# Holding halves of three streamed weight granules in freed PSUM banks, in a recurrent attention kernel

## The chip, the cores and the metric

The kernel runs on 1 core of one Trainium2 chip. The time is device microseconds of one execution on that core; lower is better. A median is over all runs of a kernel in one comparison. A ratio is the mean time of one kernel's fast runs over that of the other's fast runs of the same rounds, so it is not quite the ratio of the medians quoted beside it; the brackets are its 95% interval. Profiles are of single executions. Their spans can lie some way from the median: the profile of before is of a run of 2164.8 us.

## The reference, cut to what matters

```python
def _A_ref(x, mem0, Wq, Wk, Wv, Wo, seg_len):      # x: 1 x 2048 x 1024, 32 heads of 128, bf16
    mem = mem0                                     # 8 rows
    for s in range(n_seg):                         # 64 segments of 32 rows, one after the other
        xs = x[:, s * seg_len:(s + 1) * seg_len, :]
        h = concatenate([mem, xs], axis=1)         # 40 rows
        q, k, v = h @ Wq, h @ Wk, h @ Wv           # 1024 -> 32 x 128
        p = softmax(where(mask, q @ k.T * scale, -1e9))
        o = (p @ v) @ Wo                           # 4096 -> 1024
        mem = o[:, :M, :]                          # the next segment needs these rows
        outs.append(o[:, M:, :])
    return concatenate(outs, axis=1)
# result = x + _A_ref(layernorm(x), ...) + _B_ref(layernorm(x), ...)
# _B_ref: two rows picked by a router go through a gated MLP; it makes up the tail
```

The recurrence sets the form of the kernel: every segment needs the eight memory rows of the one before, so all four weight matrices are gone through 64 times.

## The kernel before

The weights are 64 granules of 128 x 2048 bf16 (512 KB): six phases of eight for Q, K and V (each matrix in two halves of heads), then sixteen for Wo. 42 granules stay resident in SBUF. The other 22 are streamed anew in each segment through six slots. The transfer that refills a slot is issued when TensorE has used the slot's granule.

```python
PHASES = [(0, 0), (1, 0), (0, 1), (1, 1), (2, 0), (2, 1)]       # (Q, K or V; half of the heads)
streamed = set(((2 * i + 1) * NG) // (2 * n_str) for i in range(n_str))
psA = ...bufs=2 ("acc");  psL = ...bufs=2 ("accl");  psT, psS one bank each;  psO = two banks ("otp")

def fetch():                                                    # called when a granule is used up
    t = wstream.tile([P, 2048], BF16, tag="g", name="g")        # one of six slots
    nc.sync.dma_start(out=granule_out(t, what[1]), in_=granule_dram(what[1]))
...
for p, (mat, half) in enumerate(PHASES):
    PSm = psA.tile(...)                                         # accumulator of the 24 new rows + 8 memory rows
    PSl = psL.tile(...) if mat in left else None                # accumulator of left rows
    for kc in range(KC):
        Gv = granule(8 * p + kc)
        # 4 matmuls of 512 columns into PSm; 4 more into PSl where there are left rows
        used(8 * p + kc)
        for fn in hooks.pop((p, kc), []): fn()                  # smaller work hung in after a granule
```

The last eight rows of each segment ("left rows") are gathered over four segments, so that one pass serves 32 of them. By j, the number of a segment modulo 4: segments with j = 0 have the V matmuls of left rows and seven deferred granules of their output projection (WL), j = 2 and 3 have their Q and K, j = 3 begins WL, and j = 1 has none of this but the preparation of the next group's input rows. The output of a group of left rows is finished in the next j = 0 segment by three hooks. Their input rows XL use the one buffer with the tag "vm", which also holds OB, the output of the segment before, until its stores have landed.

```python
def load_left(G, queue=nc.gpsimd):
    X = one.tile([P, 512], BF16, tag="vm", name="XL")           # waits until the stores of OB have landed
    ...four transfers from x...
OB = one.tile([P, 512], BF16, tag="vm", name="OB")
...
todo += [((1, 3), left_load), ((3, 6), left_norm), ((4, 3), left_store)]   # (phase, granule of the phase)
```

`left_norm` normalises XL on VectorE. `left_store` adds it to WL on TensorE (the "residual"), copies WL out and stores it. Attention of a half of the heads (`scores`, softmax, `attend`) is hung in after granules (2,5), (4,5), (5,3), (5,6) and inside the output projection.

## Time and profile before

The median was 2148.7 us at first, and 2149.8 us (2137.5 to 2168.0) over four runs, the first three and one more. The lines of the page, of TensorE's waits and of the windows are in the prediction. Cutting the trace where ScalarE has copied OB out gives this table by kind of segment (means of 15 or 16 segments; "granules" is TensorE's idle time ended by a streamed granule, "other" all its other idle time of that sort; sums of the trace):

| j | us a segment | TensorE busy | waits: granules | waits: other | MB moved |
|---|---|---|---|---|---|
| 0 | 32.35 | 27.46 | 1.25 | 3.19 | 11.7 |
| 1 | 30.50 | 23.86 | 4.15 | 2.21 | 12.0 |
| 2 | 31.69 | 26.10 | 2.49 | 2.84 | 12.0 |
| 3 | 31.71 | 27.57 | 0.47 | 3.77 | 12.4 |

One more line of before is from the waits of VectorE (who waited for whom: us in total, times, longest), at the normalisation of XL:

```profile
DVE XL L254 <- DMA QKL<-qkl_d: 20.8, 16, 3.2
```

(As the prediction says, the name in this line is a wrong guess: what lands is XL.) So left rows came a little late, 1.3 us on average in 16 waits.

### The profile page before, as it was taken

The page shows a single profiled execution, that of the slowest core. Times are in us where ns is not written, and L with a number is a line of the kernel's source. Part 1 is how long each engine was busy: PE and PEld are TensorE (multiplying, and loading weights), DVE is VectorE, ACT ScalarE, POOL GpSimd, SP SyncE. Part 2 cuts the span into 40 slices and gives each one's busy share as a digit, 9 for nine tenths or more (in the row PEclk, how much of TensorE's full clock was granted, in tenths as well). Part 3 has the DMA queues.
Part 4 walks back from the last instruction along what each step waited for, and adds up shares of the span by engine and source line. Part 5 has one row for each costly group of instructions (what it writes and reads, how often), then busy time and mean ns, then how long its engine had stood idle before and what let it go on. Part 6 is the DMA issues. An engine that isn't in the chain of part 4 may idle for free.

```text
span 2163.1 us, 81861 instructions
## 1 busy us (share of the span) xinstructions
PE 1741.4 (81%) x36202; PEld 897.5 (41%) x36202; DVE 730.2 (34%) x2196; ACT 503.6 (23%) x1165; POOL 544.5 (25%) x1030
## 2 busy tenths in 40 slices
PE   3588888887888888788888888888888888878775
PEld 1234444444444444444444444444444444444341
DVE  5533332333333333333333333333333333233330
ACT  4512222212222222221222122222222222222220
POOL 4422212222132222223122221323222222322211
PEclk8689998999999999999999989999999999999996
DMA  9899999999999999999999999999999999999998
GB/s 359 331 387 382 384 363 352 369 364 383 369 369 393 358 379 399 386 394 386 393 380 392 375 382 386 381 398 373 389 396 389 401 372 400 369 392 350 380 381 345
DMA packets 294344, 818.22 MB, mean 378 GB/s; under 512 B 37458, under 2 KB 42770, under 8 KB 293988
## 3 DMA queue, kind: packets, MB, share of 16 engines
q1 hardware_dynamic: 267652, 782.34, 95.1%
q0 software_dynamic: 23520, 26.06, 3.6%
q8 instruction: 283, 4.64, 0.8%
q10 hardware_dynamic: 2816, 4.59, 0.6%
q14 instruction: 73, 0.60, 0.1%
HBM read 800.22 MB, written 12.59 MB: 376 GB/s over the span
## 4 chain that ended last, share of the span: by engine, by line
DMA 42%; PE 42%; DVE 6%; issue 5%; ACT 3%; POOL 2%; ACTq 0%; POOLq 0%; DVEq 0%; SPq 0%
PE PSm L563 19%; DMA g<-in_A_Wo_dram 14%; DMA g<-in_A_Wv_dram 10%; PE PSl L567 6%; DMA g<-in_A_Wq_dram 6%; PE WO L603 5%; DMA qkl_d<-QS 3%; PE WL L603 3%; PE PTq L422 2%; DMA g<-in_A_Wk_dram 1%; PE OP L512 1%; DVE SPS L472 1%; DMA XP<-in_A_x_dram 1%; DVE NM L471 1%; DMA wres<-in_A_Wo_dram 1%
## 5 line engine op out<-in xcount | busy, mean ns | idle before, releaser
L563 PE MATMUL PSm<-wres,ST 128*32 128x512 bf16 x8192 | 756.7, 399 | 22.3 <-DVE ST L302 17.9
L563 PE MATMUL PSm<-g,ST 128*32 128x512 bf16 x4096 | 422.3, 399 | 69.2 <-DMA g<-in_A_Wk_dram 25.6
L563 PEld LDWEIGHTS <-ST 128*32 128x32 bf16 x12288 | 301.0, 98 | 411.3 <-issue 170.7
L603 PEld LDWEIGHTS <-OT 128*32 128x32 bf16 x8192 | 214.8, 97 | 157.0 <-issue 139.0
L575 ACT CAST XB<-PSm 128x512 bf16<-128x512 f32 x256 | 150.4, 588 | 542.3 <-PE PSm L563 542.3
L603 PE MATMUL WO<-wres,OT 128*32 128x256 bf16 x5120 | 231.9, 278 | 15.0 <-issue 9.1
L603 PE MATMUL WO<-g,OT 128*32 128x256 bf16 x3072 | 160.3, 278 | 92.2 <-DMA g<-in_A_Wo_dram 70.0
L567 PE MATMUL PSl<-wres,STL 128*32 128x512 bf16 x2048 | 208.7, 397 | 0.0
L333 POOL DMA_DIRECT2D QKL<-qkl_d x126 | 91.9, 730 | 329.8 <-PE SPS L466 131.5
L517 ACT CAST OT<-OP 128x256 bf16<-128x256 f32 x256 | 95.4, 373 | 247.8 <-PE OP L514 247.8
L473 ACT ACTIVATE SPS<-SPS 128x320 f32<-128x320 f32 x128 | 54.0, 422 | 397.4 <-DVE SPS L472 386.5
L636 POOL DMA_DIRECT2D out_dram<-OB x256 | 129.6, 513 | 66.0 <-DVE OB L632 37.1
L422 PE MATMUL PTq<-IDENT,XB 128*128 128x128 bf16 x1024 | 103.1, 224 | 48.4 <-ACT XB L575 37.2
L454 POOL COPY KT<-QKL 128x128 bf16<-128x128 bf16 x128 | 38.3, 299 | 383.1 <-PE WO L603 301.5
L471 DVE TENSOR_REDUCE NM<-SPS 128x8 f32<-128x320 f32 x128 | 62.9, 491 | 205.6 <-PE SPS L466 205.6
L519 DVE CAST OTL<-OP 128x64 bf16<-128x64 f32 x128 | 28.7, 224 | 296.9 <-ACT OT L517 296.9
L422 PEld LDWEIGHTS <-XB 128*128 128x128 bf16 x1024 | 60.0, 98 | 152.9 <-ACT XB L575 126.6
L567 PEld LDWEIGHTS <-STL 128*32 128x32 bf16 x3072 | 84.7, 100 | 67.7 <-issue 12.7
L512 PE MATMUL OP<-PT,VM 32*128 32x40 bf16 x2048 | 92.4, 178 | 24.7 <-ACT VM L585 23.0
L512 PEld LDWEIGHTS <-VM 32*128 32x128 bf16 x2048 | 64.8, 91 | 112.0 <-ACT VM L585 49.3
L429 DVE COPY KT<-PTq 128x512 bf16<-128x512 bf16 x128 | 54.2, 424 | 164.3 <-PE PTq L422 162.7
L567 PE MATMUL PSl<-g,STL 128*32 128x512 bf16 x1024 | 104.2, 396 | 0.0
(133 smaller groups left out, 1951.3 us busy)
## 6 DMA issues: line engine op xcount, KB each, us to landing
g<-in_A_Wq_dram SPq DMA_DIRECT2D x384, 512.0 KB, 7.2
g<-in_A_Wo_dram SPq DMA_DIRECT2D x384, 512.0 KB, 7.2
g<-in_A_Wk_dram SPq DMA_DIRECT2D x320, 512.0 KB, 6.5
g<-in_A_Wv_dram SPq DMA_DIRECT2D x320, 512.0 KB, 8.0
qkl_d<-QS POOLq DMA_DIRECT2D x64, 128.0 KB, 5.9
QKL<-qkl_d POOLq DMA_DIRECT2D x126, 64.0 KB, 5.8
g<-in_B_w_gate_dram SPq DMA_DIRECT2D x16, 448.0 KB, 6.9
g<-in_B_w_up_dram SPq DMA_DIRECT2D x16, 448.0 KB, 5.8
```

Of the source, the lines that this page charges most:

```text
L333: nc.gpsimd.dma_start(out=t[:, :, :], in_=qkl_d[s // 4][:, half, :, s % 4, :].rearrange("m p c -> p m c"))
L422: nc.tensor.transpose(out=PTq[:, il, :, :].rearrange("p j r -> p (j r)"), in_=XB[:, il * P:(il + 1) * P], identity=IDENT[:, :])
L429: nc.vector.tensor_copy(out=keys(half)[:, :, 0:32], in_=pv)
L471: nc.vector.tensor_reduce(out=NM[:, :], in_=S8, axis=AX.X, op=ALU.max, negate=True)
L473: nc.scalar.activation(out=S8, in_=S8, func=ACTF.Exp, scale=SCALE)
L512: nc.tensor.matmul(o, lhsT=VM[half][q0:q0 + 32, il * P:(il + 1) * P], rhs=PTm[q0:q0 + 32, il, 0:NK], start=True, stop=False, tile_position ...
L517: nc.scalar.copy(out=OT[half][:, 2 * ph:2 * ph + 2, :, :], in_=ov[:, :, :, 0:SEG])
L563: nc.tensor.matmul(PSm[32 * jq:32 * jq + 32, :], lhsT=ST[:, kc, :], rhs=Gv[:, 512 * jq:512 * (jq + 1)], start=(kc == 0), stop=(kc == KC - ...
L567: nc.tensor.matmul(PSl[32 * jq:32 * jq + 32, :], lhsT=cur["stl"][:, kc, :], rhs=Gv[:, 512 * jq:512 * (jq + 1)], start=(kc == 0), stop=(kc ...
L575: nc.scalar.copy(out=XB[:, :], in_=PSm[:, :])
L603: nc.tensor.matmul(PS[32 * g:32 * g + 32, 0:256], lhsT=lhs(h), rhs=Gv[:, D * hs + 256 * g:D * hs + 256 * (g + 1)], start=(first and hs == ...
L636: nc.gpsimd.dma_start(out=out2[s * SEG:s * SEG + XM, 256 * g:256 * (g + 1)], in_=OB[32 * g:32 * g + XM, 0:256])
```

## The change

Its intent: save transfers. Three of the four PSUM banks that attention sums and left rows had used separately are freed, each keeps half a granule (256 KB) for the whole run, and ScalarE copies it into the slot while only the other half is transferred. To free the banks, the attention sums go into the accumulator's bank and the transposes' bank, and left rows get one bank where they had two. With one bank, WL must be out before phase 4 begins, so its normalisation and store come earlier. The diff, cut to its core (the prologue's and tail's renaming of banks is left out):

```diff
+HELD = (18, 27, 36)
...
-    psL = ...bufs=2;  psO = ...bufs=1 (two banks)
+    psL = ...bufs=1;  psC = ...bufs=1 (three banks, c0 to c2)
...
-            if what[0] == "w":
+            if what[0] == "w" and what[1] in held:
+                nc.sync.dma_start(out=t[:, 0:1024], in_=granule_dram(what[1])[:, 0:1024])
+                nc.scalar.copy(out=t[:, 1024:2048], in_=held[what[1]][:, :].bitcast(BF16))
+            elif what[0] == "w":
                 nc.sync.dma_start(out=granule_out(t, what[1]), in_=granule_dram(what[1]))
...
+            ends.append(lambda: softmax(half, S8, NM))      # exponent behind the phase's accumulator copy
+
+        def softmax(half, S8, DN):
             nc.scalar.activation(out=S8, in_=S8, func=ACTF.Exp, scale=SCALE)
...
-            OP = psO.tile([P, 2, 512], F32, tag="otp", name="OP")
+            if ph == 0:
+                OA[half] = psA.tile([P, 512], F32, tag="acc", name="OA")
+            OB1 = psT.tile([P, 4 * NK], F32, tag="t", name="OP")
+            c1 = 256 if half == 0 else 256 * ph
+            OP = (OA[half][:, c1:c1 + 4 * NK], OB1[:, :])
...
+            lag, behind = 2 if j == 0 else 0, []            # left matmuls two granules behind
...
+                if s == 0 and g in HELD:
+                    held[g] = psC.tile([P, 512], U32, tag=f"c{HELD.index(g)}", name="HELD")
+                    nc.vector.tensor_scalar(out=held[g][:, :], in0=Gv[:, 1024:2048].bitcast(U32), ...)
...
-        WO = psA.tile([P, 512], F32, tag="acc", name="WO")
+        WO = OA[0]
...
-            todo += [((1, 3), left_load), ((3, 6), left_norm), ((4, 3), left_store)]
+            todo += [((1, 3), left_load), ((2, 4), left_norm), ((3, 4), left_store)]
```

More of the change, by code (lines that the diff above doesn't have):

```diff
@@ L71 @@
     streamed = set(((2 * i + 1) * NG) // (2 * n_str) for i in range(n_str))
+    assert all(g in streamed and g < 48 for g in HELD)
     def granule_dram(g):
@@ L90 @@
     psA = ctx.enter_context(tc.tile_pool(name="psA", bufs=2, space=PSUM))
-    psL = ctx.enter_context(tc.tile_pool(name="psL", bufs=2, space=PSUM))
+    psL = ctx.enter_context(tc.tile_pool(name="psL", bufs=1, space=PSUM))
     psT = ctx.enter_context(tc.tile_pool(name="psT", bufs=1, space=PSUM))
     psS = ctx.enter_context(tc.tile_pool(name="psS", bufs=1, space=PSUM))
-    psO = ctx.enter_context(tc.tile_pool(name="psO", bufs=1, space=PSUM))
+    psC = ctx.enter_context(tc.tile_pool(name="psC", bufs=1, space=PSUM))
     qkl_d = [dram.tile([2, 2, P, 4, P], BF16, name=f"qkl_d{t}") for t in range(NT)]
@@ L196 @@
     res_tiles = {}
+    held = {}
     def fetch():
@@ L397 @@
             VL = one.tile([P, 1024], BF16, tag="vl", name="VL")
-        QT, KT, QKL, PTs, OT, nxt = {}, {}, {}, {}, {}, {}
+        QT, KT, QKL, PTs, OT, OA, nxt = {}, {}, {}, {}, {}, {}, {}
         hooks = {}
+        ends = []
         def hook(p, kc, fn):
@@ L472, in scores @@
             nc.vector.tensor_tensor(out=S8, in0=S8, in1=NM[:, :].unsqueeze(2).to_broadcast([P, 8, NK]), op=ALU.add)
+            ends.append(lambda: softmax(half, S8, NM))
+        def softmax(half, S8, DN):
             nc.scalar.activation(out=S8, in_=S8, func=ACTF.Exp, scale=SCALE)
-            DN = NM
             nc.vector.tensor_reduce(out=DN[:, :], in_=S8, axis=AX.X, op=ALU.add)
@@ L510, in attend @@
                     c0 = half * 512 + il * P
-                    o = OP[:, jl, il * NK:(il + 1) * NK]
+                    o = OP[jl][:, il * NK:(il + 1) * NK]
                     nc.tensor.matmul(o, lhsT=VM[half][q0:q0 + 32, il * P:(il + 1) * P], rhs=PTm[q0:q0 + 32, il, 0:NK],
@@ L515, in attend @@
                                      start=False, stop=True, tile_position=(q0, 0), skip_group_check=True)
-            ov = OP[:, :, 0:4 * NK].rearrange("p a (i q) -> p a i q", i=4)
-            nc.scalar.copy(out=OT[half][:, 2 * ph:2 * ph + 2, :, :], in_=ov[:, :, :, 0:SEG])
             h0 = 16 * half + 8 * ph
-            (nc.scalar.copy if half == 0 else nc.vector.tensor_copy)(
-                out=OTL[:, h0:h0 + 8, j, :].rearrange("p (a i) r -> p a i r", a=2), in_=ov[:, :, :, SEG:NK])
+            for jl in range(2):
+                ov = OP[jl].rearrange("p (i q) -> p i q", i=4)
+                copy = nc.vector.tensor_copy if half == 1 and jl == 1 else nc.scalar.copy
+                copy(out=OT[half][:, 2 * ph + jl, :, :], in_=ov[:, :, 0:SEG])
+                copy(out=OTL[:, h0 + 4 * jl:h0 + 4 * jl + 4, j, :], in_=ov[:, :, SEG:NK])
         for pk, fn in todo:
@@ L564 @@
                                      start=(kc == 0), stop=(kc == KC - 1), tile_position=(0, 32 * jq))
-                if PSl is not None:
+                if s == 0 and g in HELD:
+                    held[g] = psC.tile([P, 512], U32, tag=f"c{HELD.index(g)}", name="HELD")
+                    nc.vector.tensor_scalar(out=held[g][:, :], in0=Gv[:, 1024:2048].bitcast(U32), scalar1=0, scalar2=None,
+                                            op0=ALU.bitwise_or)
+                if PSl is None:
+                    used(g)
+                else:
+                    behind.append((kc, Gv))
+                while behind and (len(behind) > lag or kc == KC - 1):
+                    kl, Gl = behind.pop(0)
                     for jq in range(4):
-                        nc.tensor.matmul(PSl[32 * jq:32 * jq + 32, :], lhsT=cur["stl"][:, kc, :],
-                                         rhs=Gv[:, 512 * jq:512 * (jq + 1)], start=(kc == 0), stop=(kc == KC - 1),
+                        nc.tensor.matmul(PSl[32 * jq:32 * jq + 32, :], lhsT=cur["stl"][:, kl, :],
+                                         rhs=Gl[:, 512 * jq:512 * (jq + 1)], start=(kl == 0), stop=(kl == KC - 1),
                                          tile_position=(0, 32 * jq))
-                used(g)
+                    used(8 * p + kl)
                 for fn in hooks.pop((p, kc), []):
@@ L583 @@
                 c0 = half * 512
+                if PSl is not None:
+                    nc.scalar.copy(out=VL[:, c0:c0 + 512], in_=PSl[:, :])
                 VM[half] = one.tile([P, 512], BF16, tag="vm", name="VM")
                 nc.scalar.copy(out=VM[half][:, :], in_=PSm[:, :])
-                if PSl is not None:
-                    nc.scalar.copy(out=VL[:, c0:c0 + 512], in_=PSl[:, :])
+            while ends:
+                ends.pop(0)()
         assert not hooks
@@ L679 @@
         for fh in range(2):
-            GU[w, fh] = (psA, psL)[w].tile([P, 512], F32, tag=("acc", "accl")[w], name="GU")
+            GU[w, fh] = psA.tile([P, 512], F32, tag="acc", name="GU") if w == 0 else \
+                psC.tile([P, 512], F32, tag=f"c{fh}", name="GU")
         for kc in range(KC):
@@ L710 @@
     nc.vector.tensor_copy(out=HT[:, :, :, :], in_=PTh.rearrange("p i (q r) -> p i q r", q=4)[:, :, :, 0:2])
-    YP = psO.tile([P, 2, 512], F32, tag="otp", name="YP")
+    YP = [psC.tile([P, 512], F32, tag="c2", name="YP"), psL.tile([P, 512], F32, tag="accl", name="YP")]
     for i in range(FC // 2):
@@ L717 @@
             for dh in range(2):
-                nc.tensor.matmul(YP[0:2, dh, :], lhsT=HT[:, 4 * fh + b, q, :],
+                nc.tensor.matmul(YP[dh][0:2, :], lhsT=HT[:, 4 * fh + b, q, :],
                                  rhs=Gt[:, a * D + dh * 512:a * D + (dh + 1) * 512],
@@ L722 @@
     NEW = fin.tile([2, D], BF16, name="NEW")
-    nc.vector.scalar_tensor_tensor(out=NEW.rearrange("p (a d) -> p a d", a=2), in0=YP[0:2, :, :], scalar=SIG[:, 0:1],
-                                   in1=OUTR.rearrange("p (a d) -> p a d", a=2), op0=ALU.mult, op1=ALU.add)
+    for dh in range(2):
+        c = slice(512 * dh, 512 * (dh + 1))
+        nc.vector.scalar_tensor_tensor(out=NEW[:, c], in0=YP[dh][0:2, :], scalar=SIG[:, 0:1], in1=OUTR[:, c],
+                                       op0=ALU.mult, op1=ALU.add)
     for c in range(2):
```

## The prediction

> **What bounds the kernel now.** I read the page from the top, then the chain of waits, the waits of TensorE, and windows cut where one segment's output is copied out. The page first:
>
> ```profile
> span 2163.1 us, 81861 instructions
> PE 1741.4 (81%) x36202; PEld 897.5 (41%) x36202; DVE 730.2 (34%) x2196; ACT 503.6 (23%) x1165; POOL 544.5 (25%) x1030
> ...
> DMA  9899999999999999999999999999999999999998
> ...
> q1 hardware_dynamic: 267652, 782.34, 95.1%
> ...
> DMA 42%; PE 42%; DVE 6%; issue 5%; ACT 3%; POOL 2%; ACTq 0%; POOLq 0%; DVEq 0%; SPq 0%
> ```
>
> The transfer engines are nearly always busy, 95.1% of them with the weight queue. Yet the chain that ended last is split evenly between transfers and TensorE, so both limits are close. How often TensorE itself waits for a streamed granule is in its waits (who waited for whom: us, times, longest):
>
> ```profile
> PE WO L603 <- DMA g<-in_A_Wo_dram: 70.0, 124, 1.8
> ...
> PE PSm L563 <- DMA g<-in_A_Wk_dram: 25.6, 52, 1.8
> ...
> PE PSm L563 <- DMA g<-in_A_Wv_dram: 21.2, 47, 1.2
> ...
> PE PSm L563 <- DMA g<-in_A_Wq_dram: 18.1, 40, 1.4
> ```
>
> These sum to 134.9 us in 263 waits: direct waiting is only 6% of the span. The windows give 115.6 us up to the end of segment 0, 1987.6 us for the other 63 segments (381 GB/s) and 59.9 us for the tail: 31.55 us a segment. Four segments in a row, j = 0, 1, 2, 3 (columns: stretch, us, busy and count of PE, PEld, DVE, ACT, POOL, clock, DMA share, GB/s):
>
> ```profile
> 1477.60:1508.70 31.10, 26.77 (x612) 14.73 (x603) 10.30 (x33) 7.49 (x18) 10.50 (x21) 1.00 1.00 356
> 1508.70:1539.90 31.20, 23.51 (x481) 11.47 (x481) 10.90 (x34) 6.16 (x16) 8.15 (x17) 1.00 1.03 401
> 1539.90:1570.40 30.50, 25.41 (x547) 13.16 (x547) 10.10 (x31) 7.65 (x18) 6.58 (x14) 1.00 1.01 378
> 1570.40:1599.50 29.10, 26.59 (x597) 14.32 (x598) 10.86 (x31) 7.24 (x17) 6.48 (x14) 1.00 1.03 412
> ```
>
> The j = 1 segment moves 401 GB/s: transfers set its pace. The j = 0 segment, which has left rows and deferred projections, moves only 356: there TensorE sets it. Averaged over all segments of a kind the windows give 32.4, 30.5, 31.7 and 31.7 us.
>
> [...] VectorE's half of OB waits for ScalarE's half of the same bank 32 times, 124.5 us. [...]
>
> **The change, part by part.**
>
> Held halves. Of 22 granules of 512 KB a segment streams, three come as 256 KB. 3 x 0.262 = 0.786 MB less a segment; a segment now moves 1987.6 x 381 / 63 = 12.02 MB, so 6.5% less. Rows become 2 KB rather than 4 KB; Wo already has 2 KB rows, and its granules land in 7.2 us, as those of Wq do, so I charge nothing. At today's 381 GB/s 11.23 MB take 29.5 us, at 400 they take 28.1. If transfers alone mattered: 2.07 x 63 = 130 us saved.
>
> Copies. From 266 ns for 128 columns (OB) and 588 for 512 (XB) a column costs 0.84 ns: 588 + 512 x 0.84 = 1.02 us each, 3.1 us a segment, about 195 us more on ScalarE, which is busy 23%: 32% after it. They are issued after granules 1, 10 and 18, that is at kc 1, 2 and 2 of phases 0, 1 and 2, five or more granules ahead of the next accumulator copy. A granule takes TensorE 0.22 us when fed (starts of successive groups in the timeline), so 1.1 us are there: these copies should hardly delay anything.
>
> Attention sums. Each attend had two evacuations (373 and 218-224 ns) and gets four of some 266 and 191 ns (my estimate for 32 columns from the same slope). For half 0 all four are on ScalarE: 0.91 us in place of 0.59; the second attend, three granules later, may wait some 0.3 us. WO now lies in the bank that ScalarE is still reading for half 0, so its residual waits for the first two of these copies, some 0.4 us. Half 1 gets shorter, as both engines copy. Together 0 to 0.7 us a segment on TensorE, 0.2 where it sets the pace on average; nothing where transfers do.
>
> Exponent behind the accumulator copy. It frees XB by up to 0.4 us in phases 2 and 4; the wait of the transposes for XB is 37.2 us in all. I take 15 us back, 0.2 us a segment, which cancels the line above.
>
> Left rows with one bank. This is the part I fear. WL must be out before phase 4, so the normalisation moves from granule (3,6) to (2,4) and the store from (4,3) to (3,4), but the load stays at (1,3). Its transfers cannot start until the four OB stores have landed, since both use one buffer. POOL and VectorE in that j = 0 segment, and when TensorE begins scores of half 0, the hook after (2,4) (start, us, engine, line):
>
> ```profile
> 1478.19 2.03 POOL L636 DMA_DIRECT2D out_dram<-OB  x4 [0.55 <-DVE OB L632]
> ...
> 1485.23 2.00 POOL L245 DMA_DIRECT2D XL<-in_A_x_dram  x4 [3.30 <-PE PSm L563]
> ```
>
> ```profile
> 1493.70 0.28 DVE L254 TENSOR_SCALAR XL<-XL,SC 128x256 bf16<-128x256 bf16 x1 [1.89 <-DMA QKL<-qkl_d]
> ```
>
> ```profile
> 1486.52 0.19 PE L461 MATMUL SPS<-KT,QT 128*32 128x40 bf16 x4
> ```
>
> The XL rows land about 15.6 us into the segment (loads at 1485.2 to 1486.7, up to 6.7 us to landing), and VectorE already waits 1.9 us for them (the name QKL in the bracket is a wrong guess; the load of XL is what lands then). After the change it waits from about 1486.3, some 7 us, with the maxima of half 0 and the copies of Q and K queued behind. TensorE reaches (3,4) at about 1489.9 and needs the normalised rows: it stops until some 1494.9, 5 us. Then VectorE works off the softmax of half 0 (3.7 us: 0.49, 0.50, the exponent 0.55, 0.49, 0.20, 0.42, 0.21, 0.43, 0.40) before Q of half 1, so the transposes at (4,1) stop for another 2 us. From (4,1) to the end took 15 us with 1.7 us of waits. So j = 0 costs about 34.5 us, 2 to 3 more than now, in 15 segments. j = 1 has such a load too, but its normalisation stays at (3,6); it can't fall much below 27 us.
>
> **The sum.** TensorE's side: 31.55 less the 134.9 / 63 = 2.1 us of waits for granules gives 29.4 us; a wait also adds the tail of an isolated group to busy time (0.40 us alone, 0.22 in a row): 263 x 0.18 / 63 = 0.7 us, so 28.7. XL adds 6 us of stop in one of four segments: +1.4, of which slower-paced phases hide a little: about 29.9. The transfers' side: 28.1 to 29.5. Six slots, some 8 us of lead, let transfers run on while TensorE stands, so the two add up only partly; two limits so close never reach either, and I take 30.3 us. Saved: 1.25 x 63 = 79 us. Prologue (three VectorE copies, one left bank) and tail: unchanged within 3 us. 2148.7 - 79 = 2070 us.
>
> **Rivals.** (a) Transfers alone bound it and the stops hide in the slots' lead: 130 us saved, 2019 us. For it: DMA share 1.00 and more in most segments, and a stop of 7 us is shorter than the lead. Against it: 361 GB/s on average in j = 0 segments. (b) TensorE and its feeders bound it: the three copies, the XL stop and shared banks eat the gain, and TensorE's waits for granules turn into waits for XL and Q: 10 to 40 us saved, 2110 to 2140. For it: direct waits are only 135 us, and j = 3 segments have hardly any (0.5 us). (c) The in-order ScalarE becomes the feeder that is late: a held copy waits for its slot, and XB behind it. Against it: the copy follows the very granule that frees the slot, and ScalarE has three quarters of its time free; I give it little.
>
> **Range and chances.** Between (a) near-complete and the mild end of (b): 2030 to 2110. The 2% line is at 2105.7. Faster 0.86, same 0.13, slower 0.01.
>
> **What would show it.** Weight queue 782 to about 733 MB (3 x 63 x 0.262 = 49.5). A row of 189 ScalarE copies of about 1.02 us. VectorE's waits ahead of XL in j = 0 growing to some 6 us each, about 90 us in all, and TensorE waiting on POOL's XL at the residual of WL, 3 to 5 us each, where it is 5.4 us in all now. j = 0 segments near 34.5 us, j = 1 near 27.5, the others near 29 to 30. TensorE's direct waits for granules falling from 135 to 50 us or less. The prediction is wrong if 2 KB rows lower the rate, if XL lands much earlier than 15 us into the segment, if the slots' lead swallows the stops (a), or if held copies delay XB.

## The result, and the profile after

The changed kernel took 2217.1 us (2210.0 to 2227.9, four runs) beside 2149.8 us for the kernel before: ratio 1.031 [1.022, 1.040], **slower by 3.1%**. Executions over 1.5% slower than the fastest of the same kernel are left out of the means. The prediction was 2070, with 2030 to 2110. Its outputs passed the comparison.

The page of after, the lines that answer to those of before (span; engines; DMA share in forty slices; weight queue with packets, MB and share; the chain that ended last):

```profile
span 2208.3 us, 82817 instructions
...
PE 1764.8 (80%) x36202; PEld 900.5 (41%) x36202; DVE 752.3 (34%) x2328; ACT 705.9 (32%) x1738; POOL 543.0 (25%) x1030
...
DMA  9899999989999999999999999999999999899989
...
q1 hardware_dynamic: 267652, 732.79, 90.8%
...
PE 42%; DMA 38%; DVE 7%; issue 6%; ACT 4%; POOL 3%; ACTq 0%; DVEq 0%; POOLq 0%; SPq 0%
```

The bytes fell by 49.5 MB as planned, ScalarE rose to 32% as planned, and the span still grew. In the chain POOL went from 2 to 3%, VectorE from 6 to 7%. The waits of TensorE name what is new (us in total, times, longest):

```profile
PE OA L632 <- DMA g<-in_A_Wo_dram: 70.1, 127, 1.8
PE WL L302 <- POOL XL L263: 47.4, 14, 7.6
...
PE PSm L581 <- DMA g<-in_A_Wq_dram: 26.9, 39, 2.0
...
PE PSm L581 <- DMA g<-in_A_Wk_dram: 8.8, 22, 1.2
...
PE PSm L581 <- DMA g<-in_A_Wv_dram: 5.5, 14, 0.9
```

The residual of WL waits 47.4 us for normalised left rows, where it was 5.4. The waits for granules sum to 111.3 us, where they were 134.9; those in the output projection did not move (70.0 and 70.1). VectorE waits for the same rows ahead of that:

```profile
DVE XL L261 <- DMA XL<-in_A_x_dram: 67.5, 19, 8.7
```

The four segments that the prediction showed, after the change (stretch, us, busy and count of PE, PEld, DVE, ACT, POOL, granted clock, DMA share, GB/s):

```profile
1501.90:1536.30 34.40, 28.98 (x620) 15.27 (x608) 10.60 (x35) 10.72 (x27) 10.34 (x21) 0.88 0.86 285
1536.30:1567.70 31.40, 24.58 (x481) 11.55 (x481) 11.22 (x36) 9.32 (x25) 8.13 (x17) 0.95 1.02 378
1567.70:1600.00 32.30, 26.96 (x548) 13.64 (x548) 10.70 (x33) 10.92 (x28) 6.68 (x14) 0.95 0.96 351
1600.00:1631.30 31.30, 26.98 (x606) 15.06 (x610) 10.91 (x32) 10.35 (x26) 6.37 (x13) 0.97 1.01 383
```

Two things are to be seen. The j = 0 segment (first line) has become the longest, its clock fell to 0.88 and its transfers to 285 GB/s. And the other three did not get clearly shorter, though each moves fewer bytes: the rate fell with the bytes. Averaged over all segments:

| j | before, us | after, us | predicted, us | clock before, after | waits for granules before, after |
|---|---|---|---|---|---|
| 0 | 32.35 | 35.10 | 34.5 | 0.98, 0.91 | 1.25, 0.58 |
| 1 | 30.50 | 30.69 | 27.5 | 0.95, 0.95 | 4.15, 4.01 |
| 2 | 31.69 | 31.51 | 29 to 30 | 0.98, 0.97 | 2.49, 1.89 |
| 3 | 31.71 | 31.96 | 29 to 30 | 0.96, 0.95 | 0.47, 0.37 |

The difference of the spans is 2208.3 - 2163.1 = 45.2 us. The segments account for it: 15 x 2.75 = 41.3 from j = 0, and 16 x (0.19 - 0.18 + 0.25) = 4.2 from the rest. The medians are 67 us apart, so this pair of profiles shows two thirds of the measured loss; the other 22 us, 0.35 us a segment, are not in the table.

Now the stop itself, in the first of those four segments. First POOL's issues of the XL load, then VectorE at the normalisation, then TensorE (start, us, engine, line, operation, and in brackets the idle time before it and what ended it):

```profile
1509.67 0.98 POOL L252 DMA_DIRECT2D XL<-in_A_x_dram  x2
```

```profile
1511.76 0.16 DVE L260 RECIPROCAL SC<-SC 128x1 f32<-128x1 f32 x1
1516.80 0.29 DVE L261 TENSOR_SCALAR XL<-XL,SC 128x256 bf16<-128x256 bf16 x1 [4.88 <-DMA XL<-in_A_x_dram]
```

```profile
1518.21 0.41 PE L302 MATMUL WL<-XL,IDENT 128*32 128x256 bf16 x4 [3.81 <-POOL XL L263]
1518.38 0.66 PE L581 MATMUL PSm<-wres,ST 128*32 128x512 bf16 x4
```

The last two XL transfers are issued at 1509.67, VectorE waits 4.88 us for them, normalises, POOL adds, and TensorE has stood for 3.81 us. VectorE's maxima of half 0 stand behind that wait: their scores were done at 1512.3, and they ran at 1517.33. The second TensorE line has something that I had not expected: a group of four matmuls takes 0.66 us, where isolated groups took 0.40. Windows of 2 us across the stop show why (columns as above; the last three are the granted clock, DMA share and GB/s):

```profile
1513.90:1515.90 2.00, 0.51 (x8) 0.10 (x5) 0.00 (x0) 0.00 (x0) 0.00 (x0) 1.00 0.96 323
1515.90:1517.90 2.00, 0.00 (x0) 0.11 (x1) 1.03 (x4) 0.00 (x0) 0.40 (x1) 0.78 1.02 398
1517.90:1519.90 2.00, 1.69 (x20) 0.86 (x23) 1.37 (x4) 0.71 (x2) 1.85 (x5) 0.50 0.93 371
1519.90:1521.90 2.00, 1.49 (x16) 0.55 (x12) 1.32 (x6) 0.58 (x1) 1.88 (x4) 0.50 0.61 127
1521.90:1523.90 2.00, 2.00 (x24) 0.66 (x22) 0.41 (x1) 0.00 (x0) 0.00 (x0) 0.51 0.59 206
1523.90:1525.90 2.00, 2.00 (x65) 1.11 (x61) 0.65 (x2) 0.00 (x0) 0.35 (x1) 1.00 0.48 109
```

The clock granted to TensorE falls to half during the stop and stays there until about 1523.9. In both traces it is either 1.00 or 0.50 and changes only on a grid of 3.41 us (they list 74 stretches of it for before, 122 for after). So a mean of 0.78 in the second window means that 44% of its 2 us were at half: the half clock began near 1517.0 and lasted some 6.8 us, two steps of the grid. TensorE did not have to stand for a whole step to lose its clock: the half clock began 2.6 us into the stop, after a step in which TensorE was still busy for 0.80 of 3.41 us. Two steps of after, then two of before, at a place where no stop of TensorE is longer than 1.35 us (columns as above):

```profile
1513.61:1517.02 3.41, 0.80 (x12) 0.44 (x9) 0.22 (x1) 0.00 (x0) 0.00 (x0) 1.00 0.99 348
1517.02:1520.43 3.41, 2.22 (x24) 0.86 (x23) 2.71 (x9) 1.15 (x3) 2.78 (x6) 0.50 0.83 330
```

```profile
1883.68:1887.09 3.41, 1.99 (x26) 0.77 (x23) 0.85 (x3) 0.58 (x1) 0.66 (x1) 1.00 1.01 338
1887.09:1890.51 3.42, 3.42 (x32) 1.23 (x35) 0.42 (x1) 0.59 (x1) 1.69 (x4) 0.50 1.02 417
```

With the 63 segments of both traces cut into such steps, full clock went over to half 86 times, and each time TensorE had been busy for 1 to 59% of the step before; no step at full clock with more was followed by half, while some with as little as 46% were not either. So a stop of some 1.5 us, or a few short ones, can cost the clock here (an estimate from these shares: 41% of a step is 1.4 us). In all, these segments had 130 us at half clock before and 239 after, of which 24 and 92 in j = 0.

The DMA share shows the other half of the damage: while TensorE stands and crawls, no slot comes free, and the transfers fall to 0.61, 0.59 and 0.48 of their share. The six slots did not carry them over the stop.

And the row of held copies, as predicted (busy, mean ns of one; idle before them):

```profile
L220 ACT COPY g<-HELD 128x1024 bf16<-128x1024 bf16 x189 | 191.2, 1012 | 259.4 <-PE PSm L581 169.8
```

### The profile page after: what moved, and what is told of

Read it like the earlier page. It is cut to its first block, busy times and chain, and to the rows that moved or that the text cites.

```text
span 2208.3 us, 82817 instructions
## 1 busy us (share of the span) xinstructions
PE 1764.8 (80%) x36202; PEld 900.5 (41%) x36202; DVE 752.3 (34%) x2328; ACT 705.9 (32%) x1738; POOL 543.0 (25%) x1030
## 3 DMA queue, kind: packets, MB, share of 16 engines
q1 hardware_dynamic: 267652, 732.79, 90.8%
## 4 chain that ended last, share of the span: by engine, by line
PE 42%; DMA 38%; DVE 7%; issue 6%; ACT 4%; POOL 3%; ACTq 0%; DVEq 0%; POOLq 0%; SPq 0%
PE PSm L581 21%; DMA g<-in_A_Wo_dram 13%; DMA g<-in_A_Wq_dram 9%; PE PSl L594 7%; PE OA L632 4%; DMA XL<-in_A_x_dram 4%; DMA qkl_d<-QS 3%; DMA g<-in_A_Wv_dram 2%; PE PTq L430 2%; PE WL L632 2%; DMA XP<-in_A_x_dram 1%; ACT XB L602 1%; POOL XL L252 1%; PE SPS L474 1%; DMA out_dram<-OB 1%
## 5 line engine op out<-in xcount | busy, mean ns | idle before, releaser
L581 PE MATMUL PSm<-wres,ST 128*32 128x512 bf16 x8192 | 774.6, 409 | 20.4 <-DVE ST L309 17.9
L581 PE MATMUL PSm<-g,ST 128*32 128x512 bf16 x4096 | 428.8, 407 | 44.2 <-DMA g<-in_A_Wq_dram 26.9
L220 ACT COPY g<-HELD 128x1024 bf16<-128x1024 bf16 x189 | 191.2, 1012 | 259.4 <-PE PSm L581 169.8
L632 PE MATMUL OA<-wres,OT 128*32 128x256 bf16 x5120 | 235.2, 277 | 26.2 <-issue 20.9
L632 PE MATMUL OA<-g,OT 128*32 128x256 bf16 x3072 | 159.0, 278 | 74.0 <-DMA g<-in_A_Wo_dram 70.1
L535 ACT CAST OT<-OA 128x128 bf16<-128x128 f32 x256 | 67.9, 265 | 227.7 <-PE OP L529 226.3
L430 PE MATMUL PTq<-IDENT,XB 128*128 128x128 bf16 x1024 | 106.3, 229 | 43.0 <-ACT XB L602 28.1
L594 PEld LDWEIGHTS <-STL 128*32 128x32 bf16 x3072 | 87.3, 101 | 91.8 <-issue 35.1
L614 ACT CAST VM<-PSm 128x512 bf16<-128x512 f32 x128 | 77.4, 604 | 140.6 <-PE PSm L581 140.6
L535 DVE CAST OT<-OP 128x128 bf16<-128x128 f32 x128 | 37.3, 291 | 224.4 <-PE OP L529 224.4
```

The costliest lines, as they stand in the source:

```text
L220: nc.scalar.copy(out=t[:, 1024:2048], in_=held[what[1]][:, :].bitcast(BF16))
L430: nc.tensor.transpose(out=PTq[:, il, :, :].rearrange("p j r -> p (j r)"), in_=XB[:, il * P:(il + 1) * P], identity=IDENT[:, :])
L535: copy(out=OT[half][:, 2 * ph + jl, :, :], in_=ov[:, :, 0:SEG])
L581: nc.tensor.matmul(PSm[32 * jq:32 * jq + 32, :], lhsT=ST[:, kc, :], rhs=Gv[:, 512 * jq:512 * (jq + 1)], start=(kc == 0), stop=(kc == KC - ...
L594: nc.tensor.matmul(PSl[32 * jq:32 * jq + 32, :], lhsT=cur["stl"][:, kl, :], rhs=Gl[:, 512 * jq:512 * (jq + 1)], start=(kl == 0), stop=(kl ...
L614: nc.scalar.copy(out=VM[half][:, :], in_=PSm[:, :])
```

## The experiments

Two questions: is the stop the whole loss, and where did the saved transfers go? Fifteen kernels ran; each was compared with the kernel before on its own chip (medians of before: 2146.6, 2149.4, 2150.0 and 2157.2 us, in the order of the four groups below). All but e4, e10, e11, e13, e14 and e15 compute the reference. Those six are wrong; the comparison of outputs passed them as well, so its tolerance does not see such edits.

### First group: the stop and the halves apart

**e1** keeps the whole change, but gives OB another buffer, so that XL can be loaded at once at the start of the j = 0 segment.

```diff
-        OB = one.tile([P, 512], BF16, tag="vm", name="OB")
+        OB = one.tile([P, 512], BF16, tag="pt", name="OB")
-            todo += [((1, 3), left_load), ((2, 4), left_norm), ((3, 4), left_store)]
+            todo += [((0, 1), left_load), ((2, 4), left_norm), ((3, 4), left_store)]
```

> The change whole, but the output rows OB sit in another buffer, so that the left rows of the j = 0 segments are loaded at granule (0,1) rather than after the stores have landed; the stop at the residual of WL should go. Theory A (the stop, and the halved TensorE clock after it, are the whole loss, and the held halves gain next to nothing): 2110 to 2155 us, j = 0 segments from 35.1 to 31.5 us or so. Theory B (the halves are worth the forecast 80 us, and the stop ate them): 2060 to 2100. Theory C (copies or 2 KB rows cost time of their own): 2165 to 2200, j = 1 to 3 unchanged.

Measured: 2129.8 us, 0.991 [0.988, 0.994] of before. The residual's wait for XL is gone from TensorE's waits, VectorE has no wait for XL at all, and j = 0 takes 31.27 us at a clock of 0.97, down from 35.10 at 0.91. Against the changed kernel that is 0.991 / 1.031, or 3.9% less. The late left rows are the loss (e6 below shows that a small part of this gain was to be had before the change too).

**e2** holds nothing and keeps the stop; **e3** is e1 and holds nothing.

```diff
-HELD = (18, 27, 36)
+HELD = ()
```

> The change with no granule held: full transfers, no ScalarE copies, the stop still there. A: within 1% of the changed kernel, 2200 to 2235, as the halves neither gain nor cost. B: slower than the changed kernel by 30 us or more. C: faster than it by 25 us or more.

> Both edits: no stop and nothing held. A: within 1% of the early-load run, 2110 to 2160. B: slower than the early-load run by 40 us or more. C: faster than it by 25 us or more.

Measured: e2 2239.5 us, 1.040 [1.033, 1.047]; e3 2146.7 us, 1.001 [0.998, 1.003]. So the halves gain 2239.5 - 2217.1 = 22 us beside the stop and 2146.7 - 2129.8 = 17 us without it. They do gain, but a sixth to an eighth of the 130 us that the saved transfer time would have been.

**e6** is the kernel before with the early load of e1 alone (its normalisation stays where it was).

> The kernel before with the same early load of left rows in j = 0. VectorE waited there 1.3 us a segment for these rows, 20.8 us in all; TensorE waited 5.4 us. A, B, C alike: 0 to 15 us faster than before. If it is faster by over 30 us, left rows were already a bound before and part of the early-load run's gain is not the undoing of the change.

Measured: 2129.1 us, 0.993 [0.989, 0.997]. The 20.8 us of waits shown above were worth most of their size to the kernel before.

With these four the loss can be followed step by step, in ratios to before: loading XL early in the kernel before -0.7% (e6); the rest of the change without held halves, early load, +0.8% (e3 over e6); the held halves -1.0% (e1 over e3); the load put back to its late place +4.0% (after over e1). Together they make +3.1% by construction, since each step starts where the last one ends; what the runs tell is the size of each.

### Second group: what swallowed the halves' gain

**e4** tests whether the copies eat the gain. It is e1 with the half transfers and without ScalarE's copies; TensorE reads the transferred half twice instead (wrong).

```diff
-                nc.scalar.copy(out=t[:, 1024:2048], in_=held[what[1]][:, :].bitcast(BF16))
+                    cq = jq % 2 if s > 0 and g in HELD else jq      # first half read twice
```

> Wrong result on purpose. The early-load run with three granules of 256 KB, without the ScalarE copies: TensorE reads the loaded half twice. A: the copies hide; within 0.7% of the early-load run (2115 to 2145). C (copies cost time of their own): 2085 to 2110.

Measured: 2141.2 us, 0.998 [0.995, 1.000]. Without the copies it is not faster than e1 (0.991). The copies cost nothing that can be seen. But e4 lies only 0.3% under e3 (1.001), where e1 lies 1.0% under it: the 17 us of gain are uncertain by a good part of themselves.

**e7** is e1 and also loads the left rows of the j = 1 segment early, at (0,1) in place of (1,3).

> The early-load run with the j = 1 load of left rows early too, at granule (0,1). VectorE waits there for these rows at (3,6). A: 0 to 20 us faster than the early-load run, as the transfers set j = 1. If left rows hold up j = 1 as they did j = 0 after the change: 30 us or more faster.

Measured: median 2146.2 us, ratio 0.994 [0.991, 0.998]. One run of 2114.0 us lies far below the others, which makes ten of the twenty count as slow by the 1.5% rule; by the medians of all runs it is 2146.2 to 2149.4. There is no further gain: in j = 1 the left rows were not late.

**e10** asks what the transfers are worth at all. It is e3, but all 22 streamed granules are transferred by half after their first time, and the half is read twice (wrong).

```diff
+            elif what[0] == "w" and what[1] in seen:
+                nc.sync.dma_start(out=t[:, 0:1024], in_=...first half...)
```

> Wrong result on purpose. The early-load run with nothing held, but from segment 1 on all 22 streamed granules come as 256 KB and TensorE reads their first half twice: the same instructions, half the streamed bytes (5.8 MB less a segment), no copies. Theory A (TensorE and what feeds it set the pace almost as tightly as transfers): 2030 to 2100 us, that is 45 to 115 below its base of 2147. Theory B (transfers are the bound, the halves' gain was lost elsewhere): under 1900. If A, the waits for granules are gone and others stay: issue, Q and K copies, the turn of a segment.

Measured: 1871.2 us, 0.872 [0.867, 0.877], with 419 MB in place of 782 on the weight queue and its share at 68%. TensorE's waits for streamed granules of the four attention matrices fall from 161.3 us in e3 to 3.4. Its segments take 27.78, 24.26, 28.76 and 26.96 us for j = 0 to 3, 2.9 to 6.2 us less than in the kernel before: TensorE with its other feeders can go that much faster in every kind. What matters more is which other waits went as well. These are TensorE's waits called "issue" (time in which it waited for nothing that the profile shows) in e3 and in e10, one fence each:

```profile
PE OA L632 <- issue: 19.6, 19, 2.4
...
PE WL L632 <- issue: 14.8, 12, 2.9
```

```profile
PE OA L641 <- issue: 4.9, 11, 0.8
...
PE WL L641 <- issue: 3.6, 6, 0.8
```

Nothing but bytes was taken away, and issue waits fell from 39.9 to 9.8 us in all. They depend on transfers, then. The page of before has a queue for instructions (packets, MB, share of the 16 engines):

```profile
q8 instruction: 283, 4.64, 0.8%
```

TensorE ran 72,404 matmuls and weight loads, which is 256 to each of these 283 packets of 16 KB, and all 52 of its issue waits in that trace end 1.2 to 1.6 us after such a packet has landed (median 1.35). The reading: TensorE's instructions come in these packets, through the same busy engines, and where it runs through them fastest, in the output projection with eight matmuls and eight weight loads a granule, it runs out of them. In the trace of before sixteen matmuls of 256 columns took 0.61 us there, as eight of 512 columns did elsewhere, and 44.9 of TensorE's 55.8 us of issue waits are in the projection.

**e11** tests that. It is e6 with the projection written as four matmuls of 512 columns in place of eight of 256: the same columns and bytes, half the instructions (wrong).

```diff
-            for hs in range(2):
-                for g in range(4):
-                    nc.tensor.matmul(PS[..., 0:256], lhsT=lhs(2 * w + hs), rhs=Gv[:, D * hs + 256 * g:...])
+            for g in range(4):
+                nc.tensor.matmul(PS[..., 0:512], lhsT=lhs(2 * w), rhs=Gv[:, 512 * g:512 * (g + 1)])
```

> Wrong result on purpose. The kernel before with the early load, and the output projection issued as four matmuls of 512 columns a granule in place of eight of 256: the same columns streamed through TensorE, 64 matmuls and 64 weight loads fewer a segment and as many fewer for left rows. Each wait of TensorE named issue in the trace ends some 1.3 us after the landing of a 16 KB instruction fetch. If these fetches pace the dense stretches: waits named issue fall from 50 us to 15 or less and the run is 40 us or more faster than its base of 2129. If they only fill slack: under 15 us faster.

Measured: 2098.3 us, 0.976 [0.971, 0.982], which is 31 us under e6 by the medians, or 36 by the ratios (0.9930 - 0.9764 of 2149.4). Every issue wait has gone from TensorE's waits (54.0 us in e6), while TensorE's busy time fell by 7.0 us only (1727.5 to 1720.5; its weight loads, which overlap, by 138.5). On this reading the fetch of instructions costs some 30 us in this kernel; the run also takes away half of the projection's weight loads and can't tell the two apart by time alone. Of the 54.0 us, 31 came back as waits for granules (131.5 us in e6, 162.5 in e11).

### Third group: place, softmax, row length, and the early normalisation alone

**e9** is the kernel before with two hooks moved and nothing else.

```diff
-            todo += [((1, 3), left_load), ((3, 6), left_norm), ((4, 3), left_store)]
+            todo += [((1, 3), left_load), ((2, 4), left_norm), ((3, 4), left_store)]
```

> The kernel before, with one part of the change alone: the normalisation of left rows moved from (3,6) to (2,4) and their store from (4,3) to (3,4). If the stop on the left rows is the cause of the loss by itself, the kernel before slows by 40 to 100 us (2190 to 2250), j = 0 segments go from 32.4 to 35 us or more, and TensorE waits for POOL's XL some 4 us in each. If the loss needs the other parts too (shared banks, copies), it stays under 2175.

Measured: 2227.5 us in the median of four runs, 1.036 [1.031, 1.041] by the three fast ones. One line of the old kernel costs as much as the whole change did (1.031 [1.022, 1.040]). Its profiled run fell in the slow state, so only its names are read, not its times: VectorE waits for XL as in the changed kernel, and TensorE stands at the next transposes, behind VectorE's softmax.

```profile
DVE XL L254 <- DMA XL<-in_A_x_dram: 88.4, 19, 9.2
```

```profile
PE PTq L422 <- DVE NM L475: 81.5, 14, 8.8
```

**e12** asks whether the choice of granules matters. It is e1 with halves of three Wo granules, where the waits for granules were largest.

```diff
-HELD = (18, 27, 36)
+HELD = (50, 53, 59)
```

> The early-load run with the held halves taken of granules 50, 53 and 59 (Wo) rather than 18, 27 and 36: the same bytes, the same number of copies. Theory P (place decides: TensorE's waits for granules sit at the burst of Wo, 70 us in granules 50 to 62, where the six slots run dry, and a saving ahead of it is lost when the slots are full): 2075 to 2110, 20 to 55 us faster than the early-load run, waits for Wo granules under 45 us. If bytes alone count: within 0.7% of it, 2115 to 2145.

Measured: 2123.0 us, 0.988 [0.983, 0.993]; e1 stands at 0.991 [0.988, 0.994], so the two can't be told apart. Their waits can. First e1's largest, then e12's waits for granules; e12 has no wait for a Wo granule among its eleven largest:

```profile
PE OA L632 <- DMA g<-in_A_Wo_dram: 63.8, 116, 3.0
PE OA L632 <- issue: 32.3, 29, 2.8
...
PE PSm L581 <- DMA g<-in_A_Wq_dram: 26.1, 52, 2.3
```

```profile
PE PSm L582 <- DMA g<-in_A_Wq_dram: 60.0, 103, 2.5
PE PSm L582 <- DMA g<-in_A_Wk_dram: 29.4, 60, 1.9
...
PE PSm L582 <- DMA g<-in_A_Wv_dram: 22.8, 39, 1.7
```

The waits for Wo went, and those for Q, K and V grew from 57.9 to 112.2 us. The likely reading: the weights come through one queue (q1, with 95.1% of the transfer engines' time before and 90.8% after), so a transfer that needn't be made moves the next one up, TensorE runs ahead until it catches up with the queue, and waits there.

**e8** is e1 with the exponent where it was before the change (not behind the accumulator copy).

> The early-load run with the exponent issued where it was before the change, ahead of the accumulator copy. The swap took waits for XB and VM away (60.2 to 31.2 us) and added waits for VectorE's QT (21.4 to 50.8 us). My theory: neutral, within 0.7% of the early-load run (2115 to 2145). If the swap is a gain: 20 us or more slower; if a loss: 20 us or more faster.

Measured: 2130.6 us, 0.992 [0.989, 0.994], the same as e1. That part of the change is neutral.

**e5** is the kernel before with granules 18, 27 and 36 loaded as two transfers of 2 KB rows each in place of one of 4 KB rows: the same bytes.

> The kernel before with granules 18, 27 and 36 brought in two transfers of 2 KB rows each: the same bytes. If 2 KB rows of a matrix of 8 KB rows are as quick per byte: within 0.7% of before. If they are slower, and that ate the halves' gain: 1% or more slower than before.

Measured: 2172.9 us, 1.011 [1.007, 1.014]: 23 us for 189 extra transfers, 0.12 us each. Short rows or one more issue do cost, and this run can't say which. The held halves don't have the extra issue. In the trace of e1 a halved granule lands 0.63 to 0.71 us after the one before it and a full one 1.23 or more (medians by granule, where transfers follow each other closely), so the half price of the transfer is real.

### Fourth group: in which kind of segment a saved transfer counts

I had by then a theory that each kind of segment has its own limit, and that only j = 1, where TensorE waits most for granules, would gain. The rival: bytes saved anywhere count alike, or not at all. The three kernels are e3 with granules 18, 27, 36, 50, 53 and 59 halved in some kinds only, the half read twice (one kind of edit, wrong): **e13** in j = 1, **e14** in j = 0 and 3, **e15** in all.

```diff
+    def halved(g, s):
+        return s > 0 and s % 4 in (1,) and g in (18, 27, 36, 50, 53, 59)     # e13; (0, 3) in e14; all in e15
```

> Wrong result on purpose (TensorE reads a loaded half twice, no copies). The early-load run with nothing held, but granules 18, 27, 36, 50, 53 and 59 come halved in the 16 segments with j = 1 alone, the kind in which TensorE waits most for granules (77 us of 160). Theory K (kinds of segment have different limits): 35 to 60 us faster than its base of 2147, 2.2 to 3.7 us a halved segment. Rival U (every segment gives alike): the gain of a halved segment is the same as in the run with j = 0 and 3.

> Wrong result on purpose. The same six granules halved in the 31 segments with j = 0 and j = 3 alone, twice as many bytes saved. K: 10 to 35 us faster than 2147, at most 1.1 us a halved segment, less than half of what a j = 1 segment gives. U: twice the gain of the j = 1 run.

> Wrong result on purpose. The same six granules halved in all 63 segments: 99 MB less, 260 us of transfer at 381 GB/s. K: 60 to 110 us faster than 2147, about the sum of the two runs and of j = 2. If transfers were the limit everywhere: over 200 us faster.

Measured: e13 2130.9 us, 0.989 [0.984, 0.995]; e14 2131.1, 0.990 [0.984, 0.995]; e15 2091.0, 0.972 [0.965, 0.978]. Taking e3 (1.0008 of before) as the base, that is 25, 24 and 63 us. e13 halves in 16 segments and e14 in 31, so a halved segment is worth 1.55 us in j = 1 and 0.79 in j = 0 and 3. This leans to the theory, but each ratio has an interval of over half a per cent to either side, as large as half the gain, so it is not settled. The traces add a hint: beside e3, the j = 1 segments of e13 are 2.1 us shorter but its j = 2 and 3 are 1.0 and 0.5 longer, and in e14 j = 0 and 3 are 0.3 and 1.0 shorter but j = 1 is 1.0 longer. Part of what a segment saves seems to be given back by the next (single executions, and that of e3 is its fastest run).

## Why the prediction was wrong

**The stop on left rows: right, and it is the loss.** The working foresaw that XL would land too late, that VectorE would wait some 7 us with TensorE behind it, that Q of half 1 would make a second stop, and that j = 0 would take 34.5 us. Measured: VectorE waited 4.9 us in the segment shown (up to 8.7), TensorE 3.8 us and then 0.51 for Q, and j = 0 took 35.10 us. It charged 88 us for this ("+1.4" a segment in 63); e1 against after gives 86, of which some 15 were to be had before the change (e6); e9 puts the stop alone at 77 (3.6% of 2150). That the charge came so close is partly luck. Two errors inside it cancel: TensorE's stops were shorter than the 5 + 2 us foreseen (47.4 us over 15 segments is 3.2, and waits for Q come to 0.7), and the longer half clock was not foreseen. A mean clock of 0.91 in place of 0.98 over 35.1 us is 2.5 us of lost full-speed work in each j = 0 segment, an estimate from the table above.

**The held halves: the step that failed.** The prediction put it as "31.55 less the 134.9 / 63 = 2.1 us of waits for granules gives 29.4 us" for TensorE, and "At today's 381 GB/s 11.23 MB take 29.5 us, at 400 they take 28.1" for the transfers, took 30.3 us as what they do together, and expected the waits for granules to fall "from 135 to 50 us or less". They fell to 111 in the changed kernel. A saving of 79 us was expected with the stop already taken off; the halves by themselves measured 17 to 22 (e1 over e3, after over e2). The predicted 30.3 x 63 = 1909 us for the segments became 2033. By kinds nearly all of that is in j = 1, 2 and 3: each should have lost 1.7 to 3 us, and none lost more than 0.2.

The runs show two things in the place of that step. First, the saved transfer time is only worth a fraction: 17 of 130 us with three halves (e1 over e3), 63 of 260 with six (e15; 6 x 0.262 MB x 63 at 381 GB/s), 277 of 953 with all 22 (e10). It is not swallowed by the copies (e4) or the choice of granules (e12). From e3 to e1 the rate of all transfers fell with their bytes, from 385 to 351 GB/s in j = 2 for example. The likely reading is that, when a transfer is saved, the queue reaches the end of its six slots sooner and stands until TensorE frees one; no run measured that by itself. Second, waits change their names. The traces of e3 and e1 give for TensorE, in us a segment:

| j | e3: granules | issue | all waits | e1: granules | issue | all waits |
|---|---|---|---|---|---|---|
| 0 | 2.07 | 0.88 | 3.66 | 1.66 | 1.31 | 3.71 |
| 1 | 4.84 | 0.22 | 6.54 | 3.75 | 0.65 | 6.46 |
| 2 | 2.06 | 0.20 | 4.93 | 1.77 | 0.34 | 5.05 |
| 3 | 1.12 | 1.22 | 3.84 | 0.38 | 1.90 | 3.80 |

With the halves every kind waits less for granules and more for its own instructions (39.9 us in all to 65.8), and the sum stays as it was. These two executions took the same time (2136.0 and 2137.0 us), so they do not show the gain of the medians; the pair e3 and e15 (on another chip) does. Over the 63 segments, waits for granules fell there by 79 us (159 to 81), issue waits rose by 22 (39 to 61), all waits fell by 38 and the time by 31. "TensorE's side" subtracted only the waits that carry a granule's name, and took what was left as TensorE's own time, 28.7 us. It was not: with half the bytes (e10) the segments average 26.9 us, and issue waits and the waits for the keys of left rows (0.80 us a segment in j = 3 in e3, 0.01 in e10) fell together with the granules. They are waits for the transfer engines under other names.

A rival that no run separates is the clock. Over the fast runs its mean was 0.957 in the kernel before and 0.952 in e3, and with saved transfers 0.943 in e1, 0.939 in e4 and 0.938 in e15, though 0.953 in e12 and 0.962 in e10. Among the runs of one kernel, 0.01 of clock goes with 13 us in e3 and 19 in e1, so the 0.0085 between the two would be worth 11 to 16 us, about as much as the halves' measured gain (an estimate from these runs). A lower clock can also be the effect of more waiting, by the busy shares shown above; how much of the lost gain it took stays open.

**Averaging over kinds was a second error in the same step.** The prediction itself noted that j = 3 has hardly any waits for granules (0.5 us; the table of before has 4.15 for j = 1), and it still set one average of TensorE against one average of the transfers. Taking the greater in each kind (j = 0 35, j = 1 and 2 at 29.5 set by transfers, j = 3 31.2, its time less its waits for granules) gives 31.2 us on average, an estimate from the tables, and a gain of 20 us in place of 79. By this estimate, about half of what the prediction of the segments missed could be had from the trace of before; the rest lies in j = 1 to 3, where waits changed their names and the clock fell.

**The other steps.** The weight queue's 733 MB, 189 copies of 1.02 us (measured 1012 ns) and ScalarE at 32% were right. The exponent's move is neutral, as charged (e8). Attention in shared banks, one left bank, the left rows' V matmuls two granules behind (which the prediction does not price) and the rest cost 0.8% (e3 over e6), where 0 was charged; which of these parts it is was not taken apart. "2 KB rows cost nothing" is open in its small sense (e5), and not the cause: the half landed in half the time. Of the rivals, (a) is refuted by the DMA shares of 0.48 to 0.61 after the stop. (b) was nearest in its mechanism, and too mild by 77 us or more. (c) is refuted by e4.

**Open.** How the lost gain divides between the kinds' own limits, instruction fetch, small loads that come late and the clock; medians of the same kernel move by half a per cent, which is as large as most of these parts.

**A version that beats both.** e12, the change with OB in another buffer, the early load and halves of Wo granules, computes the reference by its construction and takes 2123.0 us: 1.2% under the kernel before [0.7, 1.7] and 4.2% under the changed one (0.988 over 1.031). e6 shows that more than half of that gain against before needs no held halves at all.

## What to carry to other kernels

When a buffer is freed by moving work earlier, look first at when the data of the moved work lands, and on which buffer its load waits: here one line of hooks cost 3.6% in the old kernel (e9), and another buffer with an early load took 3.9% off the changed one (e1). Don't price saved bytes by their transfer time when compute and transfers run in step through a few slots: here 13 to 29% of it came back as time, so measure it once with a kernel that transfers less and computes wrong. When a wait is taken away, ask of every wait that has another name, "issue" above all, whether the same engines are behind it: here issue waits fell from 39.9 to 9.8 us when only bytes were taken away (e10). And look at the granted clock of every run: half clock came here also where no stop of TensorE was longer than 1.35 us.
